# New unit orders and planner constants for a segment-recurrent transformer block, with small copies moved to GpSimd

## The chip, the cores and the metric

The kernel runs on one core of a Trainium2 chip. The metric is the device time in microseconds of one execution, the median of several runs. An execution has five engines with a queue of instructions each: TensorE (PE, matmul), VectorE (DVE), ScalarE (ACT), GpSimd (POOL) and SyncE (SP, which here issues DMAs). They wait for each other through semaphores alone. The profile shows one execution; its span is the time from the first to the last instruction.

## The reference

`x` is 2048 tokens of width 512 in bfloat16. Part A is attention with a recurrent memory: the layernormed tokens are cut into 64 segments of 32, and 8 memory rows stand before each. The new memory is the attention's own output at those rows, so segment s + 1 cannot begin before segment s has gone through its output projection.

```python
def _A_ref(x, mem0, Wq, Wk, Wv, Wo, seg_len):
    ...
    mask = (idx[:, None] < M) | (idx[:, None] >= idx[None, :])
    mem = mem0
    outs = []
    for s in range(n_seg):
        xs = x[:, s * seg_len:(s + 1) * seg_len, :].copy()
        h = jnp.concatenate([mem, xs], axis=1)
        q = jnp.einsum('btd,dhe->bhte', h, Wq)
        ...
        scores = jnp.einsum('bhqe,bhke->bhqk', q, k) * scale
        scores = jnp.where(mask[None, None], scores, -1000000000.0)
        p = _softmax(scores, axis=-1)
        o = jnp.einsum('bhqk,bhke->bhqe', p, v)
        o = jnp.einsum('bhte,hed->btd', o, Wo)
        mem = o[:, :M, :].copy()
        outs.append(o[:, M:, :])
    return jnp.concatenate(outs, axis=1)

h = x + _A_ref(_layernorm(x, axis=-1), A_mem0, A_Wq, A_Wk, A_Wv, A_Wo, A_seg_len)
h2 = h + _B_ref(_layernorm(h, axis=-1), B_w1, B_b1, B_w2, B_b2)
```

There are 32 heads of 128. Part B is an MLP (512 to 1792 to 512, gelu, biases) over a second layernorm, and both parts are added to the residual.

## The kernel before

**Tokens.** A segment has 40 rows, but a TensorE tile takes 32 columns of weights. So the kernel splits them: 24 of the segment's own tokens and the 8 memory rows form the 32 rows that are on the recurrent path (`hT`, pack A). The other 8 tokens of four segments, whose values depend on x alone, form a pack of 32 rows for a block of four segments (`hB`, pack B), projected one block ahead. TensorE works in four column groups of 32 (mode MC) for projections and scores, in four row groups (mode MR) for probabilities times values, and on the whole array (mode MF) for the MLP. Going from one mode to another costs time.

**Units.** Within a segment TensorE's work is cut into units. K0, K1, Q0, Q1, V0, V1 are the projections of heads 0 to 15 and 16 to 31, four units each, one per 128 rows of the weights (L796, and L547 where the loaded weights are kept). SC0 and SC1 (L963) are scores in which the memory rows and the block's other tokens ask, SA (L1025) are scores in which the 24 tokens ask. PV0 and PV1 (L994, L998) multiply probabilities and values for SC0 and SC1; PVA (L1055) does so for SA, one segment later. WO (L1083) is the output projection, eight units. F0 and F1 are fillers, off the recurrent path: projections of the next block's pack B in three of four segments, the pack's output projection (`wo_B`, L1112, eight units in F1) in the fourth, and in the last block first pieces of the MLP.

**The recurrent chain.** After WO, DVE transposes the result (L1095) and adds its two halves into the next segment's memory rows (L1089, `hT`); then that segment's Q and K units may start. ACT or DVE copies each projection out of PSUM (L814, L815), DVE transposes it (L839), a small copy puts the memory rows' queries into the matrix ZC (L853), and GpSimd puts the block's other queries beside them (L861). SC0 follows, then on DVE the maximum (L972), on ACT the exponent (L976), on DVE reciprocal (L979), product (L982) and transpose (L983), then PV0. SC1 and PV1 go the same way. ACT copies the outputs (L814, `OT`), and WO starts.

**What sets the order.** TensorE's order is written out by hand. `ORDERS` holds, for each kind of segment, a list such as `V1.3.4`: units 3 up to 4 of V1. The kinds are a1 to a3 for segments 1 to 3, z60 to z63 for the last four, and m0 to m3 for those between, by segment number modulo 4. `TURNED` names the projections that go through their four units backwards, so that a unit can keep the weights that the one before has loaded. The other engines' orders come from a planner that runs when the kernel is built (`Sched.schedule`): every operation has a duration `dur`; `lat` is the time from the end of one to the start of a dependent one (`HOP`); operations are placed by priority, the length of the chain behind them plus an entry of `BONUS` by operation and kind of segment; an operation of `either` goes to the engine on which it ends first, DVE being charged `LEAN` more. The engines then run these orders strictly. A planned time is not used on the chip, only the order that follows from it; what comes late holds all that is queued behind it on its engine.

`finalize` turns dependencies into semaphore waits. `align` pads TensorE's program with repeated weight loads so that every fourth segment begins at the same place in a block of 256 instructions (`LOCK`, `FETCH_N`):

```python
if LOCK is not None and o.tag is not None and units == SKIP + 1 and seg % 4 == 0 and seg:
    owed = (LOCK - at) % FETCH_N
```

The run has three stages: loading the weights and segment 0; segments 1 to 63; and the rest of the MLP.

## Time and profile before

| | |
|---|---|
| median of 3 runs | 807.59 us (804.5 to 808.98) |
| span of the profiled execution | 802.2 us; its whole time is not shown on the page |
| PE busy | 775.9 us (97%) |
| DVE busy | 600.7 us (75%) |
| ACT busy | 558.0 us (70%) |
| GpSimd busy | 90.1 us (11%) |
| granted TensorE clock, mean | 0.998 |
| start of segment 1 | 49.0 us |
| SC0 of segment 5, of segment 61 | 93.61 us, 672.84 us |

A row of the order of time on an engine has the start in us, the duration in us, engine, line and operation, the tiles written and read, shapes, the number of merged instructions, and in brackets the idle time before with what ended it. Four matmuls make a projection unit, and they overlap. Since a matmul's recorded end lies behind the start of the next, the busy share says little about small waits, and the distance between starts says more.

### The profile page before, as it was taken

The numbers are of one execution on the slowest core, as the hardware profiler recorded it, in microseconds if no ns is written. First come the engines' busy times: TensorE is split into PE (matmuls) and PEld (weight loads), VectorE is DVE, ScalarE is ACT, GpSimd is POOL, SyncE is SP. The second block draws the span as 40 slices with busy tenths as digits, with TensorE's granted clock in tenths as the row PEclk, the third lists the DMA queues.
The fourth block names the chain that finished last, engine by engine and source line by source line (L and its number), as shares of the span: only waits on it lengthen the run. The fifth ranks groups of instructions, "written<-read, shape, count | busy, mean of one in ns | idle before, by whom it ended". The sixth has DMA issues, their size and how long they took to land.

```text
span 802.2 us, 46835 instructions
## 1 busy us (share of the span) xinstructions
PE 775.9 (97%) x21699; PEld 423.1 (53%) x20880; DVE 600.7 (75%) x1847; ACT 558.0 (70%) x1580; POOL 90.1 (11%) x211
## 2 busy tenths in 40 slices
PE   2899999999999999999999999999999999999998
PEld 1455555555555555555555555555555555644444
DVE  3277878888888888888888888888888888732311
ACT  1557777777777777777778777777777777773342
POOL 5022000010001010101010101000000000020700
PEclk9999999999999999999999999999999999999999
DMA  9961010201111121102010202010212112074300
GB/s 367 394 174 24 4 37 11 45 12 37 26 33 30 30 33 27 36 19 42 19 43 15 49 12 50 13 37 20 50 25 56 51 38 59 17 232 127 86 27 26
DMA packets 65555, 48.77 MB, mean 61 GB/s; under 512 B 28996, under 2 KB 63308, under 8 KB 63820
## 3 DMA queue, kind: packets, MB, share of 16 engines
q1 hardware_dynamic: 65024, 45.50, 20.3%
q8 instruction: 166, 2.72, 1.4%
q14 instruction: 33, 0.27, 0.1%
q10 hardware_dynamic: 332, 0.27, 0.1%
HBM read 31.08 MB, written 8.13 MB: 49 GB/s over the span
## 4 chain that ended last, share of the span: by engine, by line
PE 91%; DMA 3%; DVE 2%; ACT 1%; SPq 1%; issue 1%; POOL 0%; DVEq 0%; ACTq 0%
PE ps L796 43%; PE ps L1083 15%; PE ps L547 8%; PE quad L1465 6%; PE ps L1451 5%; DMA WQ<-in_A_Wq_dram 3%; PE ps L1112 3%; PE quad L994 3%; PE quad L1055 2%; PE ps L1025 2%; PE ps L1233 1%; PE ps L963 1%; PE quad L963 1%; SPq L708 1%; PE quad L998 1%
## 5 line engine op out<-in xcount | busy, mean ns | idle before, releaser
L1083 PE MATMUL ps<-WO,OT 128*32 128x256 bf16 x4224 | 140.6, 274 | 0.1
L796 PE MATMUL ps<-WQ,hT 128*32 128x512 bf16 x1864 | 131.6, 379 | 0.7 <-DVE hT L1089 0.5
L796 PE MATMUL ps<-WV,hT 128*32 128x512 bf16 x1364 | 125.2, 381 | 0.0
L796 PE MATMUL ps<-WK,hT 128*32 128x512 bf16 x1700 | 123.6, 380 | 0.1
L815 ACT ACTIVATE kq<-ps 128x512 bf16<-128x512 f32 x160 | 95.4, 597 | 32.3 <-PE ps L796 26.4
L1083 PEld LDWEIGHTS ps<-WO,OT 128*32 128x32 bf16 x4224 | 100.9, 96 | 26.5 <-ACT OT L814 5.5
L814 ACT CAST kq<-ps 128x512 bf16<-128x512 f32 x162 | 94.8, 585 | 19.9 <-PE ps L796 13.1
L814 ACT CAST OT<-quad 128x128 bf16<-128x128 f32 x191 | 84.4, 442 | 27.0 <-PE quad L998 18.8
L839 DVE STREAM_TRANSPOSE KALL<-kq 128x256 f32<-128x256 f32 x160 | 71.2, 445 | 15.0 <-ACT kq L814 11.8
L796 PEld LDWEIGHTS ps<-WQ,hT 128*32 128x32 bf16 x1864 | 50.3, 97 | 58.8 <-issue 19.0
L861 POOL COPY ZC<-QTB 128x256 bf16<-128x256 bf16 x64 | 25.6, 401 | 477.2 <-PE ps L963 455.7
L796 PEld LDWEIGHTS ps<-WK,hT 128*32 128x32 bf16 x1700 | 45.8, 96 | 56.9 <-issue 14.5
L547 PE MATMUL ps<-WV,hT 128*32 128x512 bf16 x684 | 67.6, 379 | 0.0
L796 PEld LDWEIGHTS ps<-WV,hT 128*32 128x32 bf16 x1364 | 38.4, 97 | 47.3 <-issue 36.6
L839 DVE STREAM_TRANSPOSE QT<-kq 128x256 f32<-128x256 f32 x128 | 57.0, 445 | 6.5 <-ACT kq L815 1.9
L1454 ACT ACTIVATE WQ<-ps,b1t 128x512 bf16<-128x512 f32 x42 | 28.9, 688 | 46.6 <-PE ps L1451 46.6
L1095 DVE STREAM_TRANSPOSE TT<-ps 128x256 f32<-128x256 f32 x66 | 29.7, 450 | 36.3 <-PE ps L1083 36.1
L814 ACT CAST VS<-ps 128x512 bf16<-128x512 f32 x65 | 38.1, 586 | 26.6 <-PE ps L796 26.5
L814 DVE CAST VS<-ps 128x512 bf16<-128x512 f32 x63 | 41.8, 663 | 5.4 <-PE ps L796 5.4
L1541 DVE TENSOR_TENSOR WV<-quad,WV 128x512 bf16<-128x512 f32 (+1 forms) x16 | 10.5, 672 | 45.6 <-PE quad L1465 45.6
L982 DVE TENSOR_TENSOR PC<-EC,rsc 128x128 bf16<-128x128 f32 x128 | 39.7, 310 | 4.3
L1112 PE MATMUL ps<-WO,OTB 128*32 128x512 bf16 x512 | 42.1, 381 | 0.4 <-issue 0.2
(163 smaller groups left out, 1432.1 us busy)
## 6 DMA issues: line engine op xcount, KB each, us to landing
WV<-in_A_Wv_dram SPq DMA_DIRECT2D x4, 1024.0 KB, 8.5
WK<-in_A_Wk_dram SPq DMA_DIRECT2D x4, 1024.0 KB, 14.2
WQ<-in_A_Wq_dram SPq DMA_DIRECT2D x4, 1024.0 KB, 24.7
WO<-in_A_Wo_dram SPq DMA_DIRECT2D x8, 512.0 KB, 9.4
v_last<-VSB SPq DMA_DIRECT2D x60, 64.0 KB, 2.9
VBD<-v_last SPq DMA_DIRECT2D x60, 64.0 KB, 2.9
h_mid<-xr SPq DMA_DIRECT2D x16, 128.0 KB, 1.8
WK<-in_B_w_dram SPq DMA_DIRECT2D x4, 512.0 KB, 4.6
```

The costliest lines, as they stand in the source:

```text
L547: return e.add_instruction(mybir.InstMatmult(name="I-%d" % (4000000 + _kept[0]), engine=mybir.EngineType.PE, start_tensor_calc=start, stop ...
L796: ins = e.matmul(o, l, m, start=(k == 0), stop=(k == DC - 1), tile_position=(0, 32 * j), skip_group_check=True)
L814: return {"act": (lambda e: e.copy(out, src), t_act(n, ps_)), "dve": (lambda e: e.tensor_copy(out, src), 0.16 + 1.042e-3 * n * fast)}
L815: return {"act": (lambda e: e.mul(out, src, scale_), t_act(n, ps_)), "dve": (lambda e: e.tensor_scalar(out, src, scale_, None, ALU.mult), ...
L839: S.op("dve", lambda e: e.transpose(out, src), reads=[("kq", i)], writes=[key], dur=t_dve(256) + 0.02, after=after)
L982: S.op("dve", lambda e: e.tensor_tensor(PC[:, r].rearrange("p t a -> p a t"), EC[:, r], bc, ALU.mult), reads=[("EC", r), ("rsc", r)], writ ...
L1083: ins = e.matmul(ps[bank][32 * j:32 * j + 32, 0:256], lhs(slot(h)), wo_cols(h, b), start=(k == 0), stop=(k == 15), tile_position=(0, 32 * ...
L1095: S.op("dve", lambda e: e.transpose(tt.rearrange("p c q t -> p (c q t)"), ps[bank][:, 0:256]), reads=[("ps", bank)], writes=[("TT", par)], ...
L1112: ins = e.matmul(ps[bank][32 * j:32 * j + 32, :], OTB[:, bk % 2, slot(h), :], WO[:, h, :], start=(k == 0), stop=(k == 7), tile_position=(0 ...
L1451: ins = e.matmul(ps[bank][:, 0:SBT], W1[:, cc, fc * P:(fc + 1) * P], hnT_of(k)[:, cc, :], start=(cc == 0), stop=(cc == DC - 1))
L1454: S.op("act", lambda e: e.activation(gT[:, fc, :], ps[bank][:, 0:SBT], ACTF.Gelu_apprx_tanh, bias=b1t[:, fc:fc + 1], scale=1.0), reads=[(" ...
L1465: S.op("pe", lambda e: e.matmul(quad[:, t, :], lhs, W2[:, fc, :], **flags), reads=[("W2", part_of(fc))] + gT_keys(k, fc), writes=[("ps", t ...
```

## The change

Five things are different; no unit of TensorE is added or removed.

1. **Orders.** `ORDERS` and `TURNED` are new for all eleven kinds. In m0, m2 and m3 the unit V1.3.4 now stands before SC1 instead of behind it. In m3, F1 is cut in other places, and four of its units instead of three stand behind WO. In m1, SC1 comes one V unit earlier, F0 and a V unit stand between PVA, PV0 and PV1, and all eight WO units follow PV1. a1 to a3 and z60 to z63 are mixed anew.
2. **Priorities.** All of `BONUS` is new.
3. **The planner's numbers.** Durations of units and of several operations are changed in the second or third digit. `lat` has its own numbers for pairs of engines (`NEAR`), an addition after some units (`TAIL`), and a time for operations that may not overlap their neighbours (`apart`, `ALONE`). A PE unit that is held by two engines at nearly the same time is charged `TWICE`. Waits are put ahead onto earlier units with a margin of 0.02 instead of 0.1.
4. **Waits on the same engine.** Where two operations only read one PSUM bank one after the other, the second no longer waits for a semaphore of its own engine (`again`).
5. **GpSimd.** The small copy of the memory rows' queries into ZC may also run on GpSimd, and so may the product that makes PA.

A constant of the second layernorm's variance is written in another way, in the same GpSimd instruction.

```diff
-HOP = {"pe": 0.21, "act": 0.06, "dve": 0.05, "pool": 0.08, "sp": 2.0}
-SWITCH = 0.1
-OVERLAP = {"act": 0.1, "dve": 0.07, "pool": 0.05, "sp": 0.0}
+HOP = {"pe": 0.225, "act": 0.052, "dve": 0.054, "pool": 0.08, "sp": 2.0}
+NEAR = {("act", "dve"): 0.032, ("dve", "act"): 0.034, ("act", "act"): 0.034, ("dve", "dve"): 0.034, ("pool", "pool"): 0.034,
+        ("dve", "pool"): 0.063, ("act", "pool"): 0.08, ("pool", "dve"): 0.034, ("pool", "act"): 0.034, ("pool", "pe"): 0.055}
+TWICE = 0.09
+MARGIN = 0.02
+ALONE = 0.031
+SWITCH = 0.105
+TAIL = {"SC0": 0.017, "SC1": 0.043, "SA": 0.044, "PV0": 0.012, "PV1": 0.012}
+OVERLAP = {"act": 0.09, "dve": 0.08, "pool": 0.05, "sp": 0.0}
...
-          "m0": "Q0.0.2 Q1.0.1 Q0.2.4 K0.0.4 Q1.1.4 K1.0.4 SC0.0.1 V0.0.1 V1.0.2 V0.1.2 V1.2.3 V0.2.4 SC1.0.1 V1.3.4 F0.0.1 PVA.0.2 PV0.0.1 F0.1.4 WO.0.2 PV1.0.1 WO.2.8 F1.0.4 SA.0.1",
-          "m1": "K0.0.1 Q0.0.2 K0.1.2 Q0.2.4 K0.2.3 Q1.0.1 K0.3.4 Q1.1.4 K1.0.4 SC0.0.1 V1.0.1 V0.0.2 V1.1.2 V0.2.3 V1.2.3 V0.3.4 SC1.0.1 V1.3.4 F0.0.1 PVA.0.2 PV0.0.1 F0.1.4 WO.0.2 PV1.0.1 WO.2.8 F1.0.3 SA.0.1 F1.3.4",
-          "m2": "K0.0.2 Q0.0.4 K0.2.4 Q1.0.4 K1.0.4 SC0.0.1 V1.0.1 V0.0.2 V1.1.2 V0.2.3 V1.2.3 V0.3.4 SC1.0.1 V1.3.4 F0.0.2 PVA.0.2 PV0.0.1 F0.2.4 WO.0.2 PV1.0.1 WO.2.8 SA.0.1 F1.0.4",
-          "m3": "K0.0.1 Q0.0.2 K0.1.2 Q0.2.4 K0.2.4 Q1.0.4 K1.0.4 SC0.0.1 V1.0.1 V0.0.1 V1.1.2 V0.1.3 V1.2.3 V0.3.4 SC1.0.1 F1.0.1 V1.3.4 PVA.0.2 PV0.0.1 F1.1.5 WO.0.1 PV1.0.1 WO.1.8 F1.5.7 SA.0.1 F1.7.8",
...
+ORDERS = {"a1": "SC0.0.1 K0.0.1 Q0.0.1 K0.1.2 Q0.1.2 K0.2.3 Q0.2.4 K0.3.4 Q1.0.1 K1.0.1 Q1.1.3 K1.1.2 Q1.3.4 K1.2.4 V1.0.2 SC0.1.2 V0.0.3 V1.2.3 V0.3.4 SC1.0.1 PVA.0.1 V1.3.4 PVA.1.2 PV0.0.1 WO.0.2 PV1.0.1 WO.2.8 SA.0.1 F1.0.4",
...
+          "m0": "Q0.0.2 Q1.0.1 Q0.2.4 K0.0.4 Q1.1.4 K1.0.4 SC0.0.1 V1.0.1 V0.0.1 V1.1.2 V0.1.2 V1.2.3 V0.2.4 V1.3.4 SC1.0.1 F0.0.1 PVA.0.2 PV0.0.1 F0.1.4 WO.0.2 PV1.0.1 WO.2.8 F1.0.4 SA.0.1",
+          "m1": "K0.0.1 Q0.0.2 K0.1.2 Q0.2.4 Q1.0.1 K0.2.4 Q1.1.4 K1.0.4 SC0.0.1 V0.0.2 V1.0.1 V0.2.3 V1.1.2 V0.3.4 SC1.0.1 V1.2.3 PVA.0.2 F0.0.1 V1.3.4 F0.1.2 PV0.0.1 F0.2.4 PV1.0.1 WO.0.8 F1.0.4 SA.0.1",
+          "m2": "K0.0.1 Q0.0.4 K0.1.2 Q1.0.1 K0.2.4 Q1.1.3 K1.0.1 Q1.3.4 K1.1.4 SC0.0.1 V1.0.1 V0.0.1 V1.1.2 V0.1.3 V1.2.3 V0.3.4 V1.3.4 SC1.0.1 F0.0.2 PVA.0.2 PV0.0.1 F0.2.4 WO.0.2 PV1.0.1 WO.2.8 SA.0.1 F1.0.4",
+          "m3": "K0.0.1 Q0.0.2 K0.1.2 Q0.2.3 K0.2.3 Q0.3.4 K0.3.4 Q1.0.1 K1.0.1 Q1.1.4 K1.1.4 SC0.0.1 V1.0.1 V0.0.2 V1.1.2 V0.2.3 V1.2.3 V0.3.4 V1.3.4 SC1.0.1 F1.0.1 PVA.0.2 PV0.0.1 F1.1.4 WO.0.2 PV1.0.1 WO.2.8 F1.4.7 SA.0.1 F1.7.8",
...
-            if w is not None:
+            if w is not None and excl and k in w.reads and k not in w.writes:
+                again.add(w)
+            elif w is not None:
                 deps.add(w)
...
-        return HOP[p.eng]
+        if p.eng == o.eng and p in o.again:
+            return -OVERLAP[p.eng]
+        return NEAR.get((p.eng, o.eng), HOP[p.eng]) + (TAIL.get(p.tag[1], 0.0) if p.eng == "pe" and p.tag is not None else 0.0)
...
-                if p.eng == E and E not in self.self_sync:
+                if p.eng == E and (E not in self.self_sync or p in o.again):
                     continue
...
-            zc[r] = S.either({"act": (lambda e: e.copy(dst, src), 0.31), "dve": (lambda e: e.tensor_copy(dst, src), 0.25)}, reads=[("QT", r)],
+            zc[r] = S.either({"pool": (lambda e: e.tensor_copy(dst, src), 0.295), "act": (lambda e: e.copy(dst, src), 0.3), "dve": (lambda e: e.tensor_copy(dst, src), 0.23)}, reads=[("QT", r)],
...
-                 writes=[bkey], dur=0.13, mode=MC, ni=32)
+                 writes=[bkey], dur=0.1175, mode=MC, ni=32)
...
-            S.op("dve", lambda e: e.tensor_tensor(PA[:].rearrange("p a t b -> p a b t"), SA[:].rearrange("p (a b) t -> p a b t", b=2), bc2, ALU.mult),
-                 ["SA", "rsa"], ["PA"], dur=0.418)
+            def pa(e):
+                return e.tensor_tensor(PA[:].rearrange("p a t b -> p a b t"), SA[:].rearrange("p (a b) t -> p a b t", b=2), bc2, ALU.mult)
+            S.either({"dve": (pa, 0.418), "pool": (pa, 0.625)}, reads=["SA", "rsa"], writes=["PA"])
...
-            S.op("pool", lambda e: e.tensor_scalar(rs, ag[:, 1:2], 1e-5, None, ALU.add), reads=[("ag2", bk)], writes=[("rs2", bk)], dur=0.2)
+            S.op("pool", lambda e: e.tensor_scalar(rs, ag[:, 1:2], 1.00001, 1e-10, ALU.mult, ALU.add), reads=[("ag2", bk)], writes=[("rs2", bk)], dur=0.2)
```

## The prediction

> **What bounds the kernel now.** I read the page first, then the busy time of each engine in the stretch of the steady segments, then the order of time on TensorE.

> ```profile
> span 802.2 us, 46835 instructions
> ...
> q8 instruction: 166, 2.72, 1.4%
> ```

> ```profile
> 93.60:667.80 574.20, 572.83 (x18240) 318.25 (x17296) 494.83 (x1558) 439.82 (x1308) 47.07 (x119) 1.00 0.14 32
> ```

> The columns are length, then PE, PEld, DVE, ACT, POOL. TensorE is busy 572.83 of 574.20 us, DVE 494.83, ACT 439.82, GpSimd 47.07. That "busy" hides waits: a matmul's end is modelled, so a PE that stands for 0.1 or 0.2 us still overlaps its last matmul. Waits are found from starts alone: the start of a unit minus the start of the one before it, against what the same unit takes where nothing is late. Here are the starts of segment 27 (type m3) and part of 26 and 28 (m2, m0).

> ```profile
> 314.19 0.37 PE L1055 MATMUL quad<-PTA,VS 32*128 32x32 bf16 x32
> 314.40 0.30 PE L994 MATMUL quad<-PTC,VS 32*128 32x16 bf16 x16
> ...
> 321.90 0.30 PE L963 MATMUL quad<-KALL,ZC 128*32 128x64 bf16 x16
> ...
> 323.53 0.31 PE L963 MATMUL ps<-KALL,ZC 128*32 128x64 bf16 x16
> 323.65 0.40 PE L1112 MATMUL ps<-WO,OTB 128*32 128x512 bf16 x4
> 323.87 0.40 PE L796 MATMUL ps<-WV,hT 128*32 128x512 bf16 x4
> 324.20 0.37 PE L1055 MATMUL quad<-PTA,VS 32*128 32x32 bf16 x32
> 324.49 0.27 PE L994 MATMUL quad<-PTC,VS 32*128 32x16 bf16 x16
> ...
> 324.73 1.05 PE L1112 MATMUL ps<-WO,OTB 128*32 128x512 bf16 x16
> ...
> 325.93 0.27 PE L994 MATMUL quad<-PTC,VS 32*128 32x16 bf16 x16
> ...
> 327.70 0.60 PE L1112 MATMUL ps<-WO,OTB 128*32 128x512 bf16 x8
> ...
> 328.86 1.26 PE L796 MATMUL ps<-WQ,hT 128*32 128x512 bf16 x20
> ...
> 332.32 0.30 PE L963 MATMUL quad<-KALL,ZC 128*32 128x64 bf16 x16
> ...
> 335.81 0.61 PE L1083 MATMUL ps<-WO,OT 128*32 128x256 bf16 x16
> 336.36 0.26 PE L994 MATMUL quad<-PTC,VS 32*128 32x16 bf16 x16
> ...
> 337.93 1.04 PE L796 MATMUL ps<-WK,hB 128*32 128x512 bf16 x16
> ...
> 339.16 0.40 PE L796 MATMUL ps<-WK,hT 128*32 128x512 bf16 x4
> ```

> The reader is to see the milestones of a segment: SC0 at 321.90, SC1 at 323.53 (+1.63), PV0 at 324.49, PV1 at 325.93 (SC1 + 2.40), end of WO at 327.70, first unit of the next segment at 328.86, next SC0 at 332.32. This segment lasts 10.42 us. Prices: SC 0.12 (323.53 to 323.65), a projection unit 0.22, PVA 0.21 (314.19 to 314.40), a change of tiling 0.11 (323.87 to 324.20, less a unit), PV to the next unit 0.24, six WO units after PV1 1.57 (336.36 to 337.93). Two waits recur. PV0 comes 0.29 after PVA where 0.21 would do: 0.08. And the next segment cannot start before its memory rows are there: 1.16 after WO (327.70 to 328.86) in m3, 1.23 (337.93 to 339.16) in m0. The rows between SC1 and PV1, on DVE and ACT, and the memory rows' add:

> ```profile
> 323.91 0.29 DVE L972 TENSOR_REDUCE nmc<-ps 128x2 f32<-128x128 f32 x1
> ...
> 324.98 0.17 DVE L979 RECIPROCAL rsc<-smc 128x2 f32<-128x2 f32 x1
> ...
> 325.52 0.24 DVE L983 STREAM_TRANSPOSE PTC<-PC 128x64 f32<-128x64 f32 x1
> ...
> 328.42 0.39 DVE L1089 TENSOR_TENSOR hT<-TT 64x32 bf16<-64x32 f32 x2
> ```

> From SC1 (323.53) the chain maximum, exponent, reciprocal, product, transpose ends at 325.76, that is 2.23, and each step follows its predecessor within 0.05. The hop to TensorE is 0.05 (hT ends 328.81, Q starts 328.86). So PV1 cannot start before SC1 + 2.28. Today it starts at + 2.40, so it waits for nothing.

> A third loss is irregular. The same place in two m3 segments, 15 and 19:

> ```profile
> 203.63 0.60 PE L1112 MATMUL ps<-WO,OTB 128*32 128x512 bf16 x6
> 204.41 0.39 PE L1112 MATMUL ps<-WO,OTB 128*32 128x512 bf16 x2 [0.18 <-issue]
> ...
> 205.06 1.27 PE L796 MATMUL ps<-WQ,hT 128*32 128x512 bf16 x20
> ```

> ```profile
> 245.19 0.84 PE L1112 MATMUL ps<-WO,OTB 128*32 128x512 bf16 x8
> ...
> 246.34 1.26 PE L796 MATMUL ps<-WQ,hT 128*32 128x512 bf16 x20
> ```

> 1.43 us against 1.15: 0.28 lost inside a unit, with nothing that released it. The instruction queue moved 166 packets of together 2.72 MB, 16 KB each, so TensorE's program arrives in blocks; I take such a gap for a block that came late. [...]

> Steady segments, from SC0 of segment 5 to that of 61:

> ```profile
> 93.61 0.30 PE L963 MATMUL quad<-KALL,ZC 128*32 128x64 bf16 x16
> ```

> ```profile
> 672.84 0.30 PE L963 MATMUL quad<-KALL,ZC 128*32 128x64 bf16 x16
> ```

> 579.23 us for 56 segments, 41.37 for each group of four.

> **The change, part by part.** Same instructions, same units; their order, and who does a few copies, is new.

> Orders of m0, m2 and m3: the last V unit goes ahead of SC1, so SC1 is at SC0 + 1.85. The work from SC1 to PV1 shrinks: SC 0.12, one filler unit with change 0.33, PVA 0.21, PV0 0.24, three fillers 0.65, two WO units with change 0.55 (335.81 to 336.36), together 2.10 for m0 and m3 (m2, with two fillers on each side, the same). The chain needs 2.28, so PV1 will wait 0.18. What is late next is everything behind PV1. The cycle is then: start to SC0 3.46 (328.86 to 332.32), 1.85, 2.28, PV1 and six WO units 1.57, memory rows 1.16: 10.32. Now: m3 10.42, m0 1.63 + 2.41 + 1.57 + 1.23 + 3.46 = 10.30, m2 the same without the 0.07 of extra wait, 10.23. In m3 one wo_B unit moves from before PV1 to behind WO, into the shadow of the memory rows (three units and SA, now four): that is its gain of 0.10. In m0 I take 1.16 for 1.23 because the 0.07 is a DVE order; if it stays, 10.39. The 0.08 at PV0 goes, since the first softmax no longer meets the second one's maximum on DVE, but behind it PV1 waits anyway.

> Order of m1: SC1 one unit earlier (1.41), fillers between PVA, PV0 and PV1, so six changes of tiling for four. Work from SC1 to PV1: SC 0.12, a V unit with change 0.33, PVA with change 0.32, three fillers with change 0.76, PV0 0.24, two fillers with change 0.54, together 2.31, so no wait; then PV1 and all eight WO units, 1.57 + 0.44 = 2.01. Cycle 3.46 + 1.41 + 2.31 + 2.01 + 1.16 = 10.35, against 10.23 (built as m0, without its 0.07).

> Sum of a group: 3 x 10.32 + 10.35 = 41.31, against 41.18 for the regular parts now (10.30 + 10.23 + 10.23 + 10.42) and 41.37 measured. So waits for data and changes of tiling cost 14 x 0.13 = 1.8 us more, and 14 x 0.19 = 2.7 us of irregular gaps are there to be saved. Are they? Counting instructions from the alignment's anchor (106 in a block at the third unit of each m0), the block that ends in the F1 units of m1 lasts 3.49 us of work now and 3.74 after; that at m0's PV1 3.53 and 3.69, m2's 3.29 and 3.55, m3's at SA 3.63 both times; the new waits at PV1 lie inside three of them and lengthen them by 0.18. Longer blocks leave the fetch more time, so I count 2.2 of the 2.7 as saved. If none were saved, the sum would be 2.2 higher; if all, 0.5 lower. Steady segments: 1.8 - 2.2 = -0.4.

> First segments. Segment 1 now:

> ```profile
> 52.48 0.43 PE L945 MATMUL quad<-maskR,maskL 128*32 128x128 bf16 x4
> ...
> 56.83 0.26 PE L994 MATMUL quad<-PTC,VS 32*128 32x16 bf16 x16
> ```

> 4.35 from the end of K1 to PV1. After: the mask unit earlier, SC1 at 0.43 + 0.12 + 5 x 0.216 = 1.63, PV1 at 1.63 + 2.28 = 3.91: -0.4. Segments 2, 3 and 60 to 63 hold fillers in other places; between -0.4 and +0.4 each way together, I take -0.2.

> Copies of memory rows' queries (ZC) on GpSimd, from ACT or DVE:

> ```profile
> 321.08 0.30 ACT L853 COPY ZC<-QT 128x128 bf16<-128x128 bf16 x1
> ```

> ```profile
> 54.60 0.40 POOL L861 COPY ZC<-QTB 128x256 bf16<-128x256 bf16 x1 [2.32 <-PE ps L963]
> ...
> 332.25 0.51 POOL L758 COPY hT<-xT 128x384 bf16<-128x384 bf16 x1 [4.73 <-DMA xT<-xn]
> 332.70 0.30 POOL L757 COPY hB<-xT 128x128 bf16<-128x128 bf16 x1
> ```

> A copy of that size takes 0.30 on either engine. ZC is ready at 321.38, SC0 starts at 321.90: 0.5 of cover, the remaining K units. Price zero; without that cover 0.30 in each of 56 segments, 17 us. On GpSimd it stands in one queue with the QTB copies (0.40), the layernorm steps and the x-row copies; no DMA is moved. PA may move there as well (0.418 of DVE); it has until PVA. ACT and DVE get room but neither sets the end. One contact shows:

> ```profile
> 54.78 0.38 DVE L982 TENSOR_TENSOR PC<-EC,rsc 128x128 bf16<-128x128 f32 x1
> ```

> ```profile
> L982 DVE TENSOR_TENSOR PC<-EC,rsc 128x128 bf16<-128x128 f32 x128 | 39.7, 310 | 4.3
> ```

> This product of two SBUF tensors took 0.38 beside the GpSimd copy, 0.31 in the mean: at most 0.07, on the chain to PV1 if they meet; bounds 0 and 56 x 0.07 = 4 us, I take 0, as the copies belong to the projections. [...]

> The dropped waits between two readers of one bank, the changed variance term on GpSimd and the planner's numbers add no instruction: zero, covered as ACT and DVE are.

> Sum: -0.4 - 0.4 - 0.2 = -1.0 on the profiled span, 801.2. Its own whole time is not shown; the runs' median, 807.6, is 5.4 above the span, so **806.6**.

> **Rivals.** *Fetches weigh more in the runs than in this profile.* The runs spread by 4.5 us (804.5 to 808.98), more than I save. If that spread is late blocks, the median run loses the profile's 2.7 and as much as 4.5 beside it, and all of it goes: 807.6 - 7.2 + 1.8 - 0.6 = 801.6. For it: the gap at 204.41 and the longer blocks; against it: only 2.7 in the profile.

> [...]

> *GpSimd blocks the scores (the other side).* The x-row copies at 332.25 wait in GpSimd's queue for a transpose by DMA:

> ```profile
> 327.56 0.41 DVE L738 TENSOR_SCALAR xn<-xr,agg,rst 128x512 bf16<-128x512 bf16 x1 [1.00 <-POOL rst L737]
> ```

> The planner counts 1.27 + 2.0 = 3.27 from 327.97, to 331.24; they start at 332.25, 1.0 late. A ZC copy planned behind them waits too, SC0 for it, and TensorE for SC0. The lateness of 1.0 and the two copies' own 0.75 (332.25 to 333.00), less the cover of 0.5, bound it at 1.25 a group; I take 0.55, the lateness less the cover with a little of the copies, 14 x 0.55 = 7.7: 814.3. It decides from 0.36 a group (5.0 over 14). Against it: a planner that sees GpSimd taken gives the copy to ACT.

> **How the numbers follow.** Forecast 0.53, more fetch 0.26, hidden fetch 0.09, GpSimd 0.12. Half a per cent, 4.0 us, is about what a measurement here can tell from no change: faster is under 803.6, slower over 811.6. Faster: 0.26 and 0.01 of the forecast, 0.27. Slower: 0.12, and 0.06 from the forecast and the hidden fetch with the 0.07s of PC or m0 added: 0.18. Same 0.55. Range 800.5 (801.6 with about 1 for scatter) to 813, which leaves out the upper part of the GpSimd case; the likeliest case alone spans 803.5 to 810.

> **What would show it.** Right: SC1 at SC0 + 1.85 and PV1 at SC1 + 2.28 in three types, m1 with PV1 at + 2.31, groups near 41.3, few gaps inside units, ZC copies of 0.30 on GpSimd. Wrong: PV1 earlier than its chain allows, groups under 41.0 or over 41.6, SC0 late behind a GpSimd copy, PC longer than 0.31.

## The result, and the profile after

The changed kernel is slower: 811.48 us (809.36 to 813.62, 9 runs) against 807.40 for the kernel before (804.5 to 809.19, 9 runs), a ratio of 1.0064 with a 95% interval of 1.0047 to 1.0080. The forecast was 806.6. From here on a ratio is always to the kernel before, measured in turns on the same chip. Line numbers grow by 39 or 40: L796 is now L835, L963 is L1002, L983 is L1022, L1083 is L1123, L1095 is L1135.

The page of the changed kernel, its span, its busy times and its chain of waits:

```profile
span 807.6 us, 46779 instructions
...
PE 775.6 (96%) x21680; PEld 417.3 (52%) x20855; DVE 561.6 (70%) x1731; ACT 551.7 (68%) x1505; POOL 162.0 (20%) x402
...
PE 85%; DMA 5%; DVE 4%; ACT 2%; SPq 1%; issue 1%; POOL 1%; DVEq 0%; POOLq 0%
```

GpSimd took over what it was offered (162.0 us for 90.1), DVE fell from 600.7 to 561.6, and the span rose from 802.2 to 807.6. TensorE holds 85% of the chain. Where the 5.4 us lie shows when the busy time is read by stage. The stretches go from the start to SC0 of segment 1, then to SC0 of segments 5, 60 and 63, then to the end. The columns are length, then busy time of PE, PEld, DVE, ACT and POOL, the granted clock, the DMA share and GB/s. Before:

```profile
0.00:52.73 52.73, 32.27 (x590) 17.80 (x769) 20.27 (x48) 20.14 (x48) 14.72 (x50) 0.97 0.94 350
52.73:93.61 40.88, 39.70 (x1271) 21.89 (x1226) 33.29 (x108) 29.45 (x91) 7.38 (x19) 1.00 0.12 20
93.61:662.36 568.75, 567.38 (x18044) 314.97 (x17096) 490.01 (x1542) 435.52 (x1292) 46.67 (x118) 1.00 0.14 32
662.36:693.85 31.49, 31.49 (x917) 17.93 (x909) 25.89 (x83) 24.14 (x71) 1.59 (x4) 1.00 0.17 47
693.85:802.22 108.37, 105.09 (x898) 50.51 (x886) 31.28 (x68) 48.76 (x81) 19.70 (x20) 1.00 0.32 93
```

After:

```profile
0.00:53.59 53.59, 32.60 (x597) 17.34 (x756) 20.38 (x47) 19.93 (x48) 14.02 (x54) 0.97 0.92 344
53.59:95.75 42.16, 39.01 (x1260) 21.76 (x1239) 31.88 (x102) 28.11 (x86) 11.13 (x30) 1.00 0.10 20
95.75:665.67 569.92, 568.83 (x18044) 311.39 (x17098) 457.29 (x1443) 429.93 (x1224) 110.98 (x284) 1.00 0.12 32
665.67:697.86 32.19, 29.89 (x899) 16.86 (x884) 24.21 (x76) 23.38 (x66) 4.87 (x13) 1.00 0.17 46
697.86:807.60 109.74, 105.30 (x896) 49.90 (x882) 27.86 (x66) 50.39 (x84) 21.03 (x23) 1.00 0.34 91
```

No stage became shorter: +0.86, +1.28, +1.17, +0.70 and +1.37, together 5.38. The steady stage, on which most of the prediction was spent, holds a fifth of it.

In that stage the milestones of an m3 segment (27) came where they were forecast. The order of time on TensorE after:

```profile
323.65 0.30 PE L1002 MATMUL quad<-KALL,ZC 128*32 128x64 bf16 x16
...
325.50 0.29 PE L1002 MATMUL ps<-KALL,ZC 128*32 128x64 bf16 x16
...
327.76 0.26 PE L1033 MATMUL quad<-PTC,VS 32*128 32x16 bf16 x16
...
330.50 1.28 PE L835 MATMUL ps<-WQ,hT 128*32 128x512 bf16 x20
...
333.96 0.31 PE L1002 MATMUL quad<-KALL,ZC 128*32 128x64 bf16 x15
```

SC1 stands at SC0 + 1.85, PV1 at SC1 + 2.26, and the next SC0 at + 10.31; forecast were 1.85, 2.28 and 10.32. PV1 waits as foreseen. In m1 (segment 25) it does not fit:

```profile
304.34 0.29 PE L1002 MATMUL ps<-KALL,ZC 128*32 128x64 bf16 x16
...
306.72 0.27 PE L1033 MATMUL quad<-PTC,VS 32*128 32x16 bf16 x16
```

PV1 stands at SC1 + 2.38 where 2.31 was forecast without a wait, in nearly all m1 segments. The medians from SC0 to SC0, before and after: m0 10.30 and 10.32, m1 10.24 and 10.41, m2 10.23 and 10.36, m3 10.43 and 10.31.

### The profile page after: what moved, and what is told of

Read it like the earlier page. It is cut to its first block, busy times and chain, and to the rows that moved or that the text cites. A ratio compares the mean times of both kernels' runs of the same rounds, so it can differ in the third digit from the quotient of the medians.

```text
span 807.6 us, 46779 instructions
## 1 busy us (share of the span) xinstructions
PE 775.6 (96%) x21680; PEld 417.3 (52%) x20855; DVE 561.6 (70%) x1731; ACT 551.7 (68%) x1505; POOL 162.0 (20%) x402
## 3 DMA queue, kind: packets, MB, share of 16 engines
q8 instruction: 166, 2.72, 1.4%
## 4 chain that ended last, share of the span: by engine, by line
PE 85%; DMA 5%; DVE 4%; ACT 2%; SPq 1%; issue 1%; POOL 1%; DVEq 0%; POOLq 0%
PE ps L835 41%; PE ps L1123 15%; PE ps L586 8%; PE ps L1491 5%; PE quad L1505 4%; DMA WQ<-in_A_Wq_dram 3%; PE quad L1033 3%; PE ps L1152 2%; PE quad L1095 2%; PE ps L1064 2%; ACT EC L1015 1%; PE ps L1002 1%; DMA WQ<-h_mid 1%; DVE PC L1021 1%; PE quad L1002 1%
## 5 line engine op out<-in xcount | busy, mean ns | idle before, releaser
L1123 PE MATMUL ps<-WO,OT 128*32 128x256 bf16 x4224 | 137.9, 274 | 1.0 <-issue 0.6
L835 PE MATMUL ps<-WQ,hT 128*32 128x512 bf16 x1804 | 133.2, 379 | 1.9 <-DVE hT L1129 1.9
L835 PE MATMUL ps<-WK,hT 128*32 128x512 bf16 x1688 | 125.2, 380 | 0.3 <-DVE hT L1129 0.2
L1123 PEld LDWEIGHTS ps<-WO,OT 128*32 128x32 bf16 x4224 | 101.2, 96 | 27.0 <-DVE rsc L1018 10.9
L835 PE MATMUL ps<-WV,hT 128*32 128x512 bf16 x1272 | 113.8, 382 | 0.0
L853 ACT CAST kq<-ps 128x512 bf16<-128x512 f32 x162 | 94.6, 584 | 16.7 <-PE ps L835 10.6
L892 POOL COPY ZC<-QT 128x128 bf16<-128x128 bf16 x128 | 37.4, 292 | 312.2 <-DVE QT L878 312.1
L853 ACT CAST OT<-quad 128x128 bf16<-128x128 f32 (+1 forms) x161 | 77.7, 483 | 24.4 <-PE quad L1037 24.2
L835 PEld LDWEIGHTS ps<-WQ,hT 128*32 128x32 bf16 x1804 | 47.0, 96 | 62.5 <-issue 25.2
L835 PEld LDWEIGHTS ps<-WK,hT 128*32 128x32 bf16 x1688 | 45.0, 96 | 55.8 <-issue 11.3
L878 DVE STREAM_TRANSPOSE QT<-kq 128x256 f32<-128x256 f32 x128 | 55.8, 437 | 18.2 <-ACT kq L854 17.1
L1135 DVE STREAM_TRANSPOSE TT<-ps 128x256 f32<-128x256 f32 x66 | 29.7, 450 | 47.3 <-PE ps L1123 46.5
L853 ACT CAST VS<-ps 128x512 bf16<-128x512 f32 x80 | 46.8, 586 | 18.6 <-PE ps L835 16.7
L835 PEld LDWEIGHTS ps<-WV,hT 128*32 128x32 bf16 x1272 | 36.1, 97 | 44.3 <-issue 27.7
L1082 POOL TENSOR_TENSOR PA<-SA,rsa 128x256 bf16<-128x256 f32 x63 | 39.2, 622 | 78.8 <-DVE rsa L1078 78.8
L1076 ACT ACTIVATE SA<-SA 128x256 f32<-128x256 f32 x64 | 26.7, 417 | 37.6 <-DVE SA L1075 35.9
L1015 ACT ACTIVATE EC<-ps,nmc 128x64 f32<-128x64 f32 x130 | 39.7, 311 | 5.8 <-DVE nmc L1011 1.6
```

Source lines behind the costliest of these rows:

```text
L835: ins = e.matmul(o, l, m, start=(k == 0), stop=(k == DC - 1), tile_position=(0, 32 * j), skip_group_check=True)
L853: return {"act": (lambda e: e.copy(out, src), t_act(n, ps_)), "dve": (lambda e: e.tensor_copy(out, src), 0.16 + 1.042e-3 * n * fast)}
L878: S.op("dve", lambda e: e.transpose(out, src), reads=[("kq", i)], writes=[key], dur=t_dve(256) + 0.02, after=after)
L892: zc[r] = S.either({"pool": (lambda e: e.tensor_copy(dst, src), 0.295), "act": (lambda e: e.copy(dst, src), 0.3), "dve": (lambda e: e.tens ...
L1015: ins = e.activation(EC[:, r, sl, :], o[:, 64 * sl:64 * sl + 64], ACTF.Exp, bias=nmc[:, r, sl:sl + 1], accum_out=smc[:, r, sl:sl + 1])
L1082: return e.tensor_tensor(PA[:].rearrange("p a t b -> p a b t"), SA[:].rearrange("p (a b) t -> p a b t", b=2), bc2, ALU.mult)
```

## The experiments

Two theories stood at the start. By the first the loss is regular: the waits at PV1 and the longer m1, 14 groups of it. By the second it comes from ends and edges: the new priorities reorder the other engines' queues in the first and last segments.

**The parts by themselves.** `all_old` takes the orders and priorities of before and keeps the rest of the change (GpSimd copies, planner's numbers, dropped waits). `head_old`, `steady_old` and `last_old` are the changed kernel with orders and priorities of before in segments 0 to 3, in m0 to m3, and in z60 to z63 alone. The core of the edits, for `all_old` and then, in the same way for their kinds alone, the others:

```diff
-BONUS = {"": -46.84, "EC0": 0.09, "EC0@a1": 48.99, "EC0@a2": -40.35, "EC0@a3": 40.03, "EC0@m0": -3.31, "EC0@m1": 4.78, "EC0@m2": -40,
+BONUS = {"": 3.88, "EC0": 19.37, "EC0@a1": -40, "EC0@a2": 0, "EC0@a3": 2.13, "EC0@m0": 4.48, "EC0@m1": 40, "EC0@m2": 0, "EC0@m3": -7.71,
...
-          "m0": "Q0.0.2 Q1.0.1 Q0.2.4 K0.0.4 Q1.1.4 K1.0.4 SC0.0.1 V1.0.1 V0.0.1 V1.1.2 V0.1.2 V1.2.3 V0.2.4 V1.3.4 SC1.0.1 F0.0.1 PVA.0.2 PV0.0.1 F0.1.4 WO.0.2 PV1.0.1 WO.2.8 F1.0.4 SA.0.1",
+          "m0": "Q0.0.2 Q1.0.1 Q0.2.4 K0.0.4 Q1.1.4 K1.0.4 SC0.0.1 V0.0.1 V1.0.2 V0.1.2 V1.2.3 V0.2.4 SC1.0.1 V1.3.4 F0.0.1 PVA.0.2 PV0.0.1 F0.1.4 WO.0.2 PV1.0.1 WO.2.8 F1.0.4 SA.0.1",
...
```

> The changed kernel with every unit order and every priority of the kernel before; the GpSimd copies, the second reader's dropped waits and the planner's new numbers stay. Theory A (the orders and priorities cost the time, place by place; GpSimd and the numbers cost nothing): 807.4 us, the kernel before, within 1.5. Rival G (the copies on GpSimd, or the numbers, cost it): 811.5.

> Orders of a1 to a3 and priorities of segments 0 to 3 as before, the rest as changed. The changed kernel is 2.15 us later at SC0 of segment 5 (0.92 in segment 0, 0.60 in segment 1, 0.75 in segment 4). Theory A: 811.5 - 2.1 = 809.4, or 810.1 if segment 4 stays late because m0 makes it so. Rival G: 811.5.

> Orders and priorities of m0 to m3 alone as before, the rest as changed. Between the starts of SC0 in segments 5 and 60 the changed kernel's profile took 1.1 us more than the kernel before's. Theory A: that comes back, 811.5 - 1.1 = 810.4, with gaps inside wo_B units again. Theory P (the recorded prediction: these orders save 0.4): 811.9. Rival G: 811.5.

> Orders and priorities of z60 to z63 as before, the rest as changed. The changed kernel's segment 60 takes 11.38 us against 10.48, and it is 1.2 later again from SC0 of segment 61 to the end. Theory A: 811.5 - 0.9 = 810.6 if only segment 60 is the orders' work, 809.4 if the end is too. Rival G: 811.5.

> The changed kernel itself, beside the next two on one chip. Its first profile had one stretch of 3.4 us at half the clock; the two kernels that shared its opening (orders of m0 to m3, or of z60 to z63, as before) had two. Theory C: the usual execution has two, SC0 of segment 1 at about 55.5 us and not 53.6; ratio 1.0064. Rival: one stretch, 53.6.

`again` is the changed kernel once more, on another chip; its ratio there is above that of the first measurement, and the two intervals do not meet.

| kernel | us | ratio | 95% |
|---|---|---|---|
| changed kernel, first chip | 811.48 | 1.0064 | 1.0047 to 1.0080 |
| `again`, another chip | 811.52 | 1.0100 | 1.0084 to 1.0116 |
| `all_old` | 806.73 | 1.0022 | 1.0011 to 1.0033 |
| `head_old` | 807.92 | 1.0036 | 1.0023 to 1.0048 |
| `steady_old` | 813.49 | 1.0099 | 1.0085 to 1.0112 |
| `last_old` | 811.71 | 1.0080 | 1.0066 to 1.0093 |

What follows: the first segments are the largest part. Taking their orders and priorities back gives 1.0036. Against `again` they make 0.64 of the 1.00 per cent (against the first measurement, 0.28 of 0.64), the last ones 0.2, which the intervals do not separate, and 0.22 is left with old orders: a part of the loss does not need the new orders at all. The four parts ran on one chip, on which the changed kernel itself did not run; if their effects add up, their ratios put it at about 1.0097 there, an estimate close to `again`.

The first theory is not refuted by `steady_old`, though its ratio stays at 1.0099. The old orders bring a loss of about 2 us of their own, the second wait shown below, so its steady stage takes 571.04. With the new orders that stage takes 569.92 (first profile) or 570.44 (`again`), 1.2 to 1.7 above before: the regular loss is real, and the smaller part.

**The first segments.** The order of time on ACT in segment 0, after and before:

```profile
39.81 0.30 ACT L1015 ACTIVATE EC<-ps,nmc 128x64 f32<-128x64 f32 x1
...
40.82 0.60 ACT L854 ACTIVATE kq<-ps 128x512 bf16<-128x512 f32 x1 [0.61 <-PE ps L835]
...
41.92 0.32 ACT L1015 ACTIVATE EC<-ps,nmc 128x64 f32<-128x64 f32 x1
```

```profile
40.84 0.32 ACT L976 ACTIVATE EC<-ps,nmc 128x64 f32<-128x64 f32 x1
...
41.41 0.61 ACT L815 ACTIVATE kq<-ps 128x512 bf16<-128x512 f32 x1
```

After, ACT stands idle 0.61 for a projection of WQ and copies it, and only then comes the exponent that PV1 needs; before, the exponent came first. What TensorE waits for in the first 56 us, after and then before (total, times, longest):

```profile
PE ps L835 <- DMA WQ<-in_A_Wq_dram: 3.2, 2, 2.1
PE quad L1033 <- DVE PTC L1022: 2.4, 2, 2.1
```

```profile
PE ps L796 <- DMA WQ<-in_A_Wq_dram: 1.1, 1, 1.1
...
PE quad L994 <- DVE rsc L979: 0.7, 1, 0.7
```

The new priorities let TensorE stand 2.1 longer for the weights, and 2.1 at PV1 in one piece; other waits shrink, so that 0.86 is left. Two edits test whether the priorities do this: `exp_first` puts the projection's copy behind the exponent, `open_old` takes only the opening's (segment 0's) priorities of before, all else as in the changed kernel.

```diff
-          "kq3@z61": 36.09, "kq3@z62": -31.94, "kq3@z63": -8.36, "kq4": -6.24, "kq4@m0": 32.64, "kq4@m1": 4.06, "kq5": -12.83, "kq5@m0": -5.62,
+          "kq3@z61": 36.09, "kq3@z62": -31.94, "kq3@z63": -8.36, "kq4": -40, "kq4@m0": 32.64, "kq4@m1": 4.06, "kq5": -12.83, "kq5@m0": -5.62,
```

> The changed kernel with one priority changed (the copies kq4 of the opening, -6.24 to -40), by which the second exponent of segment 0 stands ahead of the kq copy on ACT. Theory A: PV1 of segment 0 no longer waits 2.11 us, SA and all behind it 0.9 us earlier, ratio 1.0064 - 0.0011 = 1.0053. Rival (the opening's end is set by weights that arrive late): nothing is gained, 1.0064.

> The changed kernel with the priorities of the opening (segment 0 and what is loaded ahead of it) as before, all orders and the other priorities as changed. Theory A (the opening's priorities, by the split wait for WQ, the emptied TensorE and the late second exponent, cost 2.3 us): ratio 1.0064 - 0.0028 = 1.0036, as with the whole head put back. Rival (the orders a1 to a3 cost it): 1.0064.

`exp_first` measured 810.00, ratio 1.0070 (1.0053 to 1.0086), `open_old` 808.78, ratio 1.0062 (1.0048 to 1.0076). Both lie above what was expected for them (1.0053 and 1.0036), and only the interval of `open_old` lies wholly under that of `again`. In the profile of `exp_first` the exponent is ahead of the copy of `kq4`, and the wait at PV1 falls from 2.11 to 0.64, now for another copy of ACT's (L977). Still PV1 starts at 43.99, no earlier than the 43.49 of the changed kernel, because in that profile a stretch at half clock (next part) lies ahead of it. So the entry made most of the wait; whether taking it back alone pays is not shown. In the profile of `open_old` the opening takes 52.80, close to the 52.73 of before. Something else goes with the opening's priorities, in segment 4. There TensorE's PV0 after, and DVE's queue:

```profile
88.12 0.26 PE L1033 MATMUL quad<-PTC,VS 32*128 32x16 bf16 x16 [0.69 <-DVE PTC L1022]
```

```profile
86.09 0.52 DVE L1129 TENSOR_TENSOR opT<-TT 64x96 bf16<-64x96 f32 x2
86.62 0.17 DVE L1018 RECIPROCAL rsc<-smc 128x2 f32<-128x2 f32 x1
...
87.23 0.68 DVE L853 CAST VS<-ps 128x512 bf16<-128x512 f32 x1
87.83 0.23 DVE L1022 STREAM_TRANSPOSE PTC<-PC 128x64 f32<-128x64 f32 x1
```

An add that nobody waits for (opT, 0.52) is put before the reciprocal, and a copy of V (0.68) before the transpose. So PV0 is 0.69 late and segment 4 takes 10.99 instead of 10.24. With `open_old`, whose priorities for segment 4 are those of the changed kernel, it takes 10.32. The planner lays out the whole run in one pass; how the opening's entries reach so far was not traced. Not all of the first segments' loss is the priorities' work: segment 1 takes 0.60 longer in the first profile, nearly all of it one gap of 0.57 inside WO at 59.77, 1.42 after a program block had landed (see the late blocks); in `again`, without that gap, it takes 10.31, as before.

**The clock.** In `again` the opening takes 55.70, not 53.59, with the same queues. Its busy time in steps of 3.4 us, the length of a stretch at half clock (3.41 in the profile of before and in the first of the changed kernel; columns as above; the sixth number after the length, without the counts in brackets, is the granted clock):

```profile
31.76:35.20 3.44, 0.40 (x4) 0.10 (x4) 0.00 (x0) 0.00 (x0) 0.00 (x0) 1.00 1.03 375
35.20:38.60 3.40, 3.28 (x32) 1.29 (x36) 0.72 (x2) 1.46 (x3) 0.00 (x0) 0.50 1.10 348
...
42.02:45.50 3.48, 1.07 (x40) 0.36 (x32) 2.05 (x8) 1.91 (x9) 0.33 (x1) 1.00 1.10 348
45.50:48.90 3.40, 3.40 (x92) 2.34 (x96) 1.47 (x4) 1.09 (x4) 0.56 (x1) 0.50 0.94 286
```

Twice a step with little work on TensorE (0.40 and 1.07 of 3.4) is followed by 3.4 us at half clock, in which a unit takes 0.43 instead of 0.22. The profiles of the changed kernel on its first chip and of before each have one such stretch, at 43.2 to 46.6 and at 42.4 to 45.8; `open_old` has none. All kernels with two of them reach SC0 of segment 1 at 55.2 to 55.8; those with one or none, at 52.3 to 53.6. A stretch near 43 us costs the kernel before next to nothing: `before_70`, which has none, reaches that SC0 at 52.51, before at 52.73.

The timed runs show which is usual. Their mean granted clock is about 0.998 where the profile of the run shows one stretch and about 0.996 where it shows two; the changed kernel stands at 0.992 to 0.996 in eight of its nine runs on the first chip, all but the profiled one, and in all six of `again`. So two or more are the rule on both chips, as was expected before `again`; that the ratio would then be 1.0064 once more was not borne out.

The work of the step ahead does not settle it alone: the steps ahead of a stretch hold 0.40 and 1.07 us in `again`, 1.28 in the changed kernel's first profile, 1.77 in before, and 1.78 and 1.88 in `warmer` (shown next), but a step with 1.37 in the changed kernel's first profile was followed by full clock.

`warmer` tries to fill the first lean step with 13 units of idle work on TensorE (results unused), 4 before the third and 9 before the fourth unit of the first Q projection:

```diff
+                                if what == "Q" and b == 0 and r == 0:
+                                    n1 = len(S.pe_order)
+                                    warm(7, 13)
+                                    more = S.pe_order[n1:]
+                                    S.pe_order[n0 + 2:] = more[:4] + S.pe_order[n0 + 2:n0 + 3] + more[4:] + S.pe_order[n0 + 3:n1]
```

> The changed kernel with 13 idle matmul units (0.216 us each, 4 before the third and 9 before the fourth unit of the first Q pass of the opening), on a bank that is free, while TensorE waits for WQ. Theory C (TensorE, emptied by the split wait, is granted half the clock for a second stretch of 3.4 us in most executions): one such stretch, near 43 us, SC0 of segment 1 at 53.6 and not 55.6, ratio to the kernel before 1.004 instead of 1.0064. Rival (the stretch comes anyway, or it costs nothing): 1.0064.

It measured 810.53, 1.0077 (1.0059 to 1.0094), where 1.004 was expected. The first half-clock stretch did go, with 2.37 of work in the step that had 0.40, but another came later:

```profile
31.76:35.20 3.44, 2.37 (x44) 0.98 (x40) 0.01 (x1) 0.00 (x0) 0.00 (x0) 1.00 1.04 377
35.20:38.60 3.40, 3.10 (x56) 1.30 (x52) 1.12 (x3) 2.12 (x5) 0.29 (x1) 1.00 1.09 352
...
42.50:45.90 3.40, 1.88 (x76) 1.53 (x80) 1.56 (x5) 1.31 (x8) 0.00 (x0) 0.50 1.10 352
45.90:49.30 3.40, 3.40 (x56) 2.34 (x52) 1.26 (x4) 0.89 (x2) 0.62 (x1) 0.50 0.86 244
```

The opening takes 55.19, two stretches again, now in a row. That lean steps precede the drops is shown; that filling them pays is not, and how much work keeps the clock up is open.

**The second wait.** `all_old` has the orders of before and yet loses 2.06 in the steady stage (570.81 for 568.75). Nearly all of it (28 x 0.07) stands between the end of WO and the next segment: 1.23 in m0, m1 and m2, where before only m0 had 1.23 and the others 1.16. The program lists the reason. Before the transpose of the memory rows (TT) stood one wait in m1 and m2, in `all_old` there are two:

```
all_old    575 L1135 STREAM_TRANSPOSE TT<-ps 128x256 [waits sem_pe,sem_dve]
one_wait   583 L1135 STREAM_TRANSPOSE TT<-ps 128x256 [waits sem_pe]
```

The wait on DVE's own semaphore is for an earlier add that read TT. `one_wait` hands it to the instruction behind that add, so it is met long before:

```diff
...
-                     reads=[("TT", par)], writes=[("opA", (sx // 4) % 2, sx % 4)], dur=0.522))
+                     reads=[("TT", par)], writes=[("opA", (sx // 4) % 2, sx % 4)], dur=0.522)).alone = True
```

> The changed kernel with the orders and priorities of before (as the first run), and the sum that writes opT marked so that the DVE instruction behind it waits for it; the transposition TT of m1 and m2 then waits for TensorE alone. In the first run memory rows came 1.23 us after WO in m1 and m2, where TT waited on two engines' semaphores, and 1.16 in m3, where on one. Theory W (a second wait costs its instruction 0.07): 1.16 in m1 and m2 too, 28 x 0.07 = 2.0 us less than the first run, ratio to the kernel before 1.000. Rival G (the 0.07 comes from sharing with GpSimd): 1.23 stays, ratio 1.002.

The same place (segment 26) on TensorE and DVE in `all_old`, then in `one_wait`:

```profile
316.40 0.42 PE L1064 MATMUL ps<-KALL,QT 128*32 128x32 bf16 x32
...
317.63 0.40 PE L835 MATMUL ps<-WK,hT 128*32 128x512 bf16 x4
```

```profile
316.24 0.42 PE L1064 MATMUL ps<-KALL,QT 128*32 128x32 bf16 x32
...
317.39 0.40 PE L835 MATMUL ps<-WK,hT 128*32 128x512 bf16 x4
```

SA starts when WO is done, K when the memory rows are there: 1.23 and 1.15, with the same instructions between. The steady stage of `one_wait`:

```profile
93.53:662.26 568.73, 566.95 (x18045) 311.59 (x17131) 468.35 (x1444) 420.04 (x1225) 112.16 (x284) 1.00 0.12 32
```

568.73: the whole 2.06 is back. `one_wait` measured 805.63, ratio 1.0014 (1.0005 to 1.0024), where 1.000 was expected; its interval meets that of `all_old`, so the evidence is the profile and not the time. So the second wait on TT cost 0.07 to 0.08 each time, even though it had long been met. The same fits the 0.07 of m0 before (a second wait on TT), the 0.08 at PV0 before (PV0 waits for ACT and DVE in m0, m1 and m3 and comes 0.29 after PVA; in m2 for ACT alone, 0.21), and the 0.07 at PV1 of m1 after, where the new order makes it wait for both. These three are read from rows; no edit tested them, and on TensorE the second wait had not long been met. The traces show where the time goes: in `all_old` a semaphore instruction stands in DVE's queue at 316.63 and TT follows at 316.70, in `one_wait` there is none, and on TensorE one stands 0.08 ahead of PV0's weights in m0 and m3 before, and none in m2.

**Repairs.** Theory: the new place of m3's units is the one regular gain, and `all_old` without the second wait can take it. `one_wait_m3` adds to `one_wait` a single edit, m3's units as in the change but with its old SC1; `best` also undoes what a DVE copy did in segment 61, where SC1 waited:

```profile
674.04 0.31 PE L1002 MATMUL ps<-KALL,ZC 128*32 128x64 bf16 x16 [0.80 <-DVE KALL L878]
```

```diff
-          "m3": "K0.0.1 Q0.0.2 K0.1.2 Q0.2.4 K0.2.4 Q1.0.4 K1.0.4 SC0.0.1 V1.0.1 V0.0.1 V1.1.2 V0.1.3 V1.2.3 V0.3.4 SC1.0.1 F1.0.1 V1.3.4 PVA.0.2 PV0.0.1 F1.1.5 WO.0.1 PV1.0.1 WO.1.8 F1.5.7 SA.0.1 F1.7.8",
+          "m3": "K0.0.1 Q0.0.2 K0.1.2 Q0.2.4 K0.2.4 Q1.0.4 K1.0.4 SC0.0.1 V1.0.1 V0.0.1 V1.1.2 V0.1.3 V1.2.3 V0.3.4 SC1.0.1 F1.0.1 V1.3.4 PVA.0.2 PV0.0.1 F1.1.4 WO.0.2 PV1.0.1 WO.2.8 F1.4.7 SA.0.1 F1.7.8",
...
-          "kq1@m3": -7.99, "kq1@z60": 8.55, "kq1@z61": -40, "kq1@z62": -4.34, "kq1@z63": 1.92, "kq2": -18.82, "kq2@a1": -5.52, "kq2@a2": -2.06,
+          "kq1@m3": -7.99, "kq1@z60": 8.55, "kq1@z61": 12.69, "kq1@z62": -4.34, "kq1@z63": 1.92, "kq2": -18.82, "kq2@a1": -5.52, "kq2@a2": -2.06,
```

> The run before this one with a new order of m3: one wo_B unit moved from before PV1 to behind WO, SC1 left at SC0 + 1.63. Theory W with fetch hidden: m3 at 10.24 instead of 10.45, 14 x 0.2 = 2.8 us less, ratio 0.9965. If blocks of TensorE's program bound the group (11 blocks in about 41 us), the gap only moves: gaps inside units again, ratio 0.999 or above.

> The kernel with single waits and the new m3 order, and one priority of segment 61 raised (kq1, -40 to 12.69), so that the copy of K1 no longer comes to DVE behind the first maximum: SC1 of segment 61 stood 2.60 us behind SC0 there, 1.63 before. Expected: 0.98 us less than that kernel's 0.9991, ratio 0.998. If the tail takes it back: 0.9991.

`one_wait_m3` measured 804.04, 0.9991 (0.9981 to 1.0002), the other case of its expectation: its m3 segments last 10.44 in the mean, not 10.24, with seven gaps inside units in the steady stage. `best` measured 802.77, 0.9980 (0.9969 to 0.9991), as expected; from SC0 of segment 60 to that of 63 it takes 31.38 for 32.36. The steady stage of `best`:

```profile
93.64:659.17 565.53, 565.28 (x18044) 312.16 (x17130) 468.12 (x1443) 419.62 (x1225) 111.60 (x284) 1.00 0.12 32
```

3.22 under before and 4.39 under the changed kernel. It is also 1.65 under `one_wait_m3` (567.18), though `best` edits only segment 61: its m3 segments last 10.32 in the mean for 10.44, with fewer gaps of the kind shown next, so the 1.65 is not the edit's work. The two intervals meet: that `best` is faster than `one_wait_m3` is not shown.

**The late blocks.** The places in the steady stages where two matmuls of one unit start more than 0.26 apart were set beside the transfers of 16 KB program blocks. Three such gaps of before (start of the late matmul, distance to the one ahead of it, end of the last block's transfer and start of the next, both counted from the late matmul):

```
120.49   0.37   -1.44   +1.11
141.25   0.46   -1.25   +1.05
204.41   0.56   -1.39   +1.47
```

The last is the gap that the prediction showed. In each gap looked at, in all kernels, TensorE goes on 1.21 to 1.65 us (1.25 to 1.64 in before) after a block has landed and before the next one starts, so I take the gaps for blocks that came late. The place of the gaps bears this out: counted in TensorE's instructions from the anchor of `align`, 62 of the 63 gaps in all profiles stand within 11 of a multiple of 256, whether the anchor is 106, 70 or 234. Before has eleven, the last ten of them 5 to 100 times 256 instructions behind the first; the changed kernel has none in its steady stage. As the gaps move with the anchor of `align`, I take it to set where blocks end. `lock_off` (60) and `lock_234` (234) move it in the changed kernel to where, by my count of positions, the shortest block would be shorter; `before_70` and `best_70` (70) move it in the kernel before and in `best`, to where it would be longer.

```diff
-LOCK = 106
+LOCK = 60
```

> The changed kernel with the blocks of TensorE's program set off: the alignment's anchor 60 instead of 106, nothing else. By counting instructions and unit prices its blocks then last 2.72, 5.09, 3.60, 3.47, 5.64, 2.72, 4.76, 3.97 us and so on, where they last 3.69 or more. Theory F (a block shorter than about 3.6 us is stretched to that): 1.9 us a group, 14 x 1.9 = 27 us, ratio 1.04 (at 3.4 us 19, at 3.8 us 41), with gaps inside units at the ends of the short blocks. Rival (crossing a block is hidden, the gaps are something else): 1.0064.

> The changed kernel with the anchor 128 instructions away, 106 to 234: by the fetches' times in the runs so far its shortest blocks would last about 2.8 us. Theory F with a least time of 3.5 to 3.7 us a block: 1.7 to 2.5 us lost in each group of four segments, 24 to 35 us, ratio 1.04 to 1.05, gaps inside units. If one short block is covered by a block already in hand: 1.01 as with the anchor 106.

> The kernel before with one number changed, the anchor of the block alignment, 106 to 70; orders, priorities and unit prices untouched. Its profile lost 2.4 us between segments 5 and 61 to gaps inside units and at PVA. Theory F (a block that ends before the next has landed makes TensorE wait; with the boundaries 36 instructions later the shortest blocks are about 3.3 us and not 2.9): most of the 2.4 us comes back with no new order at all, ratio 0.997 to 0.998. Rival (the boundary plays no part): 1.000.

> The fastest kernel so far with the same number changed, 106 to 70. It still loses about 1.4 us to such gaps (m3 at 10.317 in the mean against 10.24, m1 at 10.266). Theory F: ratio 0.998 - 0.0017 = 0.9963. Rival: 0.998.

`lock_off` measured 810.08, 1.0078 (1.0059 to 1.0097): no gaps, a steady stage of 569.41, and far from the 27 us expected. `lock_234` measured 818.24, 1.0174 (1.0153 to 1.0196), a fifth of what was expected over `again`. Its steady stage, and that of the changed kernel in `again`:

```profile
98.47:672.93 574.46, 572.78 (x18044) 319.95 (x17097) 457.33 (x1443) 431.10 (x1224) 111.55 (x284) 1.00 0.15 31
```

```profile
97.24:667.68 570.44, 568.84 (x18044) 311.14 (x17098) 457.19 (x1443) 429.40 (x1224) 110.89 (x284) 1.00 0.12 32
```

4.0 us by one number, most of it in m0 (median 10.54 for 10.32), and gaps are back. That the place of the blocks costs time is shown; my sizes were wrong. The least times of a block in the expectations (3.4 to 3.8 us) were my estimates; no run shows one. `before_70` measured 803.66, 0.9986 (0.9974 to 0.9998), near the 0.997 to 0.998 expected. With nothing but this number, the gaps of m1 go (mean 10.22 for 10.29), but m3 has three of up to 1.2, so that in its profile the steady stage is only 0.2 shorter than before, and not most of 2.4. `best_70` measured 801.70 (800.75 to 802.81), 0.9970 (0.9958 to 0.9982), the fastest version; that it is faster than `best` is not shown, as the intervals meet, and its steady stage in the profile is 0.73 longer.

## Why the prediction was wrong

The forecast was 806.6, no change, and the time is 811.48, slower by 0.6 per cent. It lies in the range only by luck: the range reached to 813 for a reason (GpSimd) that did not come.

*"Add no instruction: zero"* for the planner's numbers, and no term at all for the priorities: this is the step that failed most. The priorities decide what stands in front of what in four strict queues. In the opening they put a projection's copy ahead of an exponent, in segment 4 an add ahead of a reciprocal. Segments 0 to 4 were to take 0.4 to 0.6 less and took 2.14 more (0.86 + 1.28), in `again` 3.63 more; of the 2.14, 0.57 is the gap in segment 1 and 0.7 the late reciprocal and transpose in segment 4. Taking the first segments' orders and priorities back gave 1.0036 for 1.0100. A view that bears on it was there: the waits of the first segments in the trace of before, with what stood next in ACT's queue.

*"PV1 at 1.63 + 2.28 = 3.91: -0.4"* in segment 1 failed too: PV1 stands 4.30 behind the end of K1 (before 4.35). SC1 to PV1 takes 2.67, for PV0 waits 0.35 for DVE's transpose and the WO units ahead of PV1 wait 0.41 for ACT's copy. With one engine late, the 2.28 of the steady chain did not hold there.

*"In m0 I take 1.16 for 1.23 because the 0.07 is a DVE order"*: the reason was wrong, it is a second wait, but in the changed kernel it did go (1.15 in m0). The same mechanism came up where I looked for none: *"2.31, so no wait"* in m1 measured 2.38, 14 x 0.07 = 1.0 us. The prediction laid the 0.08 at PV0 to the second maximum on DVE, the same mistake.

*Steady segments, -0.4*, measured +1.17 (`again`: +1.69). The waits for data came as worked out: 2.28 at PV1, seen 2.29 in m0 and 2.26 in m3; cycles of m0 and m3 10.32, seen 10.32 and 10.31. The second wait made m1 10.41 for 10.35, and m2 took 10.36 for 10.32 (2.32 at PV1), as in most of its segments the step from SC1 to PVA is 0.03 to 0.18 longer. There PVA starts 0.06 to 0.09 behind an ACT copy of V that ends late, because matmuls of the V unit ahead of it start late, 10 to 12 instructions into a block. In `lock_off`, where only the blocks lie elsewhere, m2 takes 10.31 in all 14 segments: so the loss goes with the place of the blocks, though these blocks had landed 2 to 3 us before, and how they act there is open. By the medians the regular terms cost 13 x 0.02 + 14 x (0.17 + 0.13 - 0.12) = 2.8 where 1.8 was forecast. What lies above the medians fell from 2.33 to 0.62, so 1.7 was saved where *"I count 2.2 of the 2.7 as saved"* stood: the large gaps went, as forecast, but the sum of the two has the other sign. Why they went is another matter than the longer blocks of the prediction: `lock_off`, whose blocks were to be shorter than any, has none either.

*"Segments 2, 3 and 60 to 63 ... -0.2"*: 60 to 62 alone cost 0.70; what follows SC0 of segment 63 cost 1.37, but kernels with old code there vary by 1.1 from one profile to another, so about 1 us of that is not settled.

*"5.4 above the span"*: a run lies about 1.8 above its own span (809.36 for 807.6). Other runs lie 1.7 to 1.8 above their own span too, so the span of before, 802.2, stands for a run of about 804.0, faster than any of its nine; this is an estimate. Most of the 5.4 was scatter between runs and not time around the span. It made the forecast of the median neither better nor worse.

*GpSimd copies: "Price zero"*: right. `one_wait`, which has them, takes 568.73 in the steady stage, before 568.75; the rival of a blocked GpSimd did not occur. The named contact did: in every m1 the product PC takes 0.37 to 0.38 beside a GpSimd copy, but PV0 does not wait for it there, so it cost nothing. From the first unit of a segment to SC0 it is 3.46 after as before. The rival in which fetches weigh more in the runs than in the profile fell too, and for the hidden fetch, to which the chances give 0.09, nothing spoke: the gaps stand at multiples of 256 instructions and move with the anchor.

## What to carry to other kernels

A table of priorities for strict queues is no free edit: price it by the operation that stands ahead of the critical one in each stage, the first and last segments above all. Count the semaphores an instruction waits for, since on DVE a second one cost 0.07 to 0.08 us even when it was met long ago, and move it to an instruction with slack. And where a program is long (here 166 blocks of 16 KB), its blocks' place is a parameter of its own: one number moved the changed kernel's steady stage by 4.0 us (574.46 for 570.44).
